# Summing the result of an attention and MLP decode step in four rows of 128 columns instead of two rows of 256

## The chip, the cores and the metric

The kernel runs on one core of a Trainium2 chip. A core has five engines with instruction queues of their own: TensorE (PE, matrix multiply, with PEld for its weight loads), VectorE (DVE), ScalarE (ACT), GpSimd (POOL) and SyncE (SP, which here only issues transfers). Transfers between HBM and the on-chip memories run on 16 DMA engines. Matmul results go to PSUM, a memory of 128 partitions in banks of 512 fp32 columns; everything else lies in SBUF, which also has 128 partitions. The metric is the device time of one execution in microseconds (us).

## What is computed

One token of width 512 goes through two branches, mixed by a gate. Branch A is attention with 32 heads of 128 over a cache of 4096 positions, branch B a small MLP with a squared ReLU. All inputs are bf16.

```python
def _A_ref(x, k_cache, v_cache, wq, wo):          # Hq = Hkv = 32, Sk = 4096, Dh = 128
    q = (x @ wq).reshape(B, Sq, Hq, Dh).transpose(0, 2, 1, 3)
    scores = jnp.einsum("bhqd,bhkd->bhqk", q, k) * (Dh ** -0.5)
    p = _softmax(scores, axis=-1)
    o = jnp.einsum("bhqk,bhkd->bhqd", p, v)
    return o.transpose(0, 2, 1, 3).reshape(B, Sq, Hq * Dh) @ wo      # wo: 4096 x 512

def _B_ref(x, w1, b1, w2, b2):                     # 512 -> 1376 -> 512
    h = x @ w1 + b1
    r = jnp.where(h > 0, h, 0)
    return (r * r) @ w2 + b2

g = _sigmoid((x * gate_w).sum(-1, keepdims=True))
return g * a + (1 - g) * b                         # 512 numbers, bf16
```

The K cache and the V cache hold 32 x 4096 x 128 bf16 numbers each, 33.5 MB.

## The kernel before

Each engine has one hand-written stream of instructions, and semaphores (`s_...`) order them. `wait_ge(s, n)` holds the engine until the semaphore has reached `n`, and `then_inc` raises it when the instruction is done (a transfer raises it by 16).

**Stream.** SyncE issues nearly all transfers on one queue, in this order: wq (L247, L248), the first K tile, w1 and w2 (L279 to L282), then K and V tiles of 4 MB in turn (`load_k`, `load_v`). There are eight groups of four heads (`NQ = 8`), each with one K tile and one V tile. A tile goes to one of three K buffers or two V buffers, and its load is issued when the buffer's last user is done. The third K buffer first holds w1, w2 and b2, so `load_k(2)` waits for the last matmul of the MLP (`s_ml`, L528). After the last V tile wo follows at L293 in four pieces, cut by `TS = [0, 20, 28, 31, 32]`: 20, 8, 3 and 1 of 32 "rows" t. Row t of wo is a 128 x 512 block.

**Scores, softmax, values.** For each group the scores are computed in three ways at once: products by GpSimd (L313) and by VectorE (L680), both summed by VectorE (L695, L689), and transposes by TensorE (L427) followed by matmuls (L441). ScalarE takes the exponentials (L358). `pv` multiplies with V into pO (L470), on four groups of partitions that begin at 0, 32, 64 and 96, and `extract` collects the heads' rows in pX.

**The result's rows.** The 512 output numbers are summed in PSUM, in a bank named pX. Before the change they lie in two places there: `accs[0]` is partitions 32 and 33, `accs[1]` partitions 0 and 1, both in columns 0 to 127. Block j (of four blocks of 128 output columns) goes to `accs[j % 2]`, as its row `j // 2`. Both rows of a place are written by each matmul: the weights are two columns, of which one is zero. The weights are cut for that from tiles of three columns with the value in the middle: `o2p` (128 x 32 x 3, the heads' outputs, of which `o2` is the middle) and `pick2` (112 x 3, ones that pick the four rows of pO). Matmuls that add into these rows are

- L520 in `mlp_out`, which puts in the scaled bias b2 (weights: `pick2`, one row);
- L535 in `mlp_cols`, which adds the MLP's rows from pvf, a copy of pO;
- L557 in `attn_rows`, for rows t = 16 to 31 of wo, four matmuls a row;
- L566 in `wide_rows`, which adds what rows t = 0 to 15 have summed in pO (L551, one matmul of 512 columns a row, on four groups of partitions) and VectorE has copied to pvf (L746).

**The end.** `busy` (L573) issues matmuls whose result nobody reads. After `regroup` (L541, with VectorE's copy into o2 at L744) come the four calls of `attn_rows`, each behind the landing of its piece of wo (`s_wo[c]`), with `wide_rows` after the first. The last matmul raises `s_acc`. Then VectorE copies `accs[0]` (L748) and ScalarE copies `accs[1]` (L385) into `ob`, partitions 32 and 33 of an SBUF tile, 256 columns, bf16. SyncE waits for both (L295), stores the two rows (L296) and waits for the store (L297).

**The start.** VectorE clears tiles, `pick2` and `o2p` among them (L636, L637), and copies the picking column into `pick2` (L640); TensorE waits for that (`s_wm`) ahead of L520.

Of the kernel before, what the change touches and what calls it, by code (L numbers as in the profile page):

```python
# [5 lines left out]
def bass_gated_mix__gqa_block_cached__dense_activation_squared_relu__decode_kernel(  # L6
# [14 lines left out]
    fp32 = mybir.dt.float32  # L21
    i32 = mybir.dt.int32
    bf16 = mybir.dt.bfloat16
    ALU = mybir.AluOpType
    ACT = mybir.ActivationFunctionType
    AX = mybir.AxisListType

    NH = 32
# [48 lines left out]
    wo_v = A_wo.rearrange("(p t) n -> p (t n)", t=32)  # L77
    w1_v = B_w1.rearrange("(p t) n -> p (t n)", t=4)
    w2_v = B_w2[0:F0, :].rearrange("(p g) n -> p (g n)", g=FG)
    out_v = out[0, 0, :].rearrange("(j p) -> j p", p=256)  # L80
    w2_x = B_w2[F1:F, :].rearrange("(q t) n -> q (t n)", t=TX)

    ctx = ExitStack()
    with ctx:
        def sb(name, shape, dt):
            return ctx.enter_context(nc.sbuf_tensor(name, shape, dt))

        def pb(name, shape, dt):
            return ctx.enter_context(nc.psum_tensor(name, shape, dt))

        def sem(name):
            return ctx.enter_context(nc.semaphore(name))
# [9 lines left out]
        kT = sb("kT", [128, NR, TC * 128], bf16)  # L102
# [9 lines left out]
        grow = sb("grow", [1, DM], bf16)  # L112
        b1r = sb("b1r", [1, F], bf16)

        ob = kT[:, 1, 0:256]
        xcol = sb("xcol", [128, 4], bf16)
        sel = sb("sel", [NH, 4, 128], bf16)
        oT = sb("oT", [NH, 128], bf16)
        o2p = sb("o2p", [128, NH, 3], bf16)
        o2 = o2p[:, :, 1]  # L120
        ident = sb("ident", [128, 128], bf16)
        identf = sb("identf", [128, 128], fp32)
        pick = sb("pick", [128, 4, 60], fp32)
        pvf = sb("pvf", [112, 512], fp32)
# [20 lines left out]
        b2r = Kt[0:1, 2, 14 * 1024:14 * 1024 + DM]  # L145
        b2g = Kt[0:1, 2, 15 * 1024:16 * 1024].bitcast(fp32)

        pick2 = sb("pick2", [112, 3], fp32)

        TT = pb("T", [128, NT * 512], fp32)  # L150
        T = [TT[:, i * 512:(i + 1) * 512] for i in range(NT)]
# [4 lines left out]
        pX = pb("pX", [128, 512], fp32)  # L156
# [5 lines left out]
        SL = pS[0:NH, 0:256].bitcast(bf16)  # L162
        H = pX[:, 160:160 + FN + TX]

        accs = [pX[32:34, 0:128], pX[0:2, 0:128]]
        O = pX[0:NH, 288:416]

        QT = pX[:, :].bitcast(bf16).rearrange("p (j d) -> p j d", d=128)
# [2 lines left out]
        def VT(i):  # L171
            return Vt[:, i % NV, :] if i < NQ - 2 else Kt[:, (i - 1) % NK, :]
# [62 lines left out]
        s_wm = sem("s_wm")  # L235
# [6 lines left out]
        s_acc = sem("s_acc")  # L242
        s_fin = sem("s_fin")
        s_out = sem("s_out")
# [5 lines left out]
        def on(engine):  # L250
            return lambda part: part(engine)

        @on(nc.sync)
        def _(eng):
            def load_k(i):
                if i >= NK:
                    eng.wait_ge(s_t, CB[i - NK + 1])
                    eng.wait_ge(s_mu, XP * (i - NK + 1))
                    eng.wait_ge(s_pm, GP * (i - NK + 1))  # L259
                if i == 2:  # L260
                    eng.wait_ge(s_ml, 1)
                eng.dma_start(Kt[:, i % NK, :], k_p[i * 128:(i + 1) * 128, :]).then_inc(s_k[i % NK], 16)

            def load_v(i):
                if i == 1:
                    eng.wait_ge(s_qr, NQ)
                    eng.wait_ge(s_h, 2)
                if i < NQ - 2:
                    if i >= NV:
                        eng.wait_ge(s_pv, i - NV + 1)  # L270
                    eng.dma_start(VT(i), v_p[i * 128:(i + 1) * 128, :]).then_inc(s_v[i % NV], 16)
                    return
                eng.wait_ge(s_t, CB[i])
                eng.wait_ge(s_mu, XP * i)
                eng.wait_ge(s_pm, GP * i)
                eng.dma_start(VT(i), v_p[i * 128:(i + 1) * 128, :]).then_inc(s_vl[i - (NQ - 2)], 16)  # L276

            load_k(0)
            eng.dma_start(w1_sb, w1_v).then_inc(s_w1, 16)  # L279
            eng.dma_start(w2a, w2_v).then_inc(s_w2, 16)  # L280
            for r in range(4):
                eng.dma_start(WX[r:QX:4, :], w2_x[r:QX:4, :]).then_inc(s_w2, 16)  # L282
            load_k(1)
            load_v(0)
            load_k(2)
            for i in range(NQ):
                if i >= 1:
                    load_v(i)
                if i + LAG < NQ:
                    load_k(i + LAG)  # L290
            eng.wait_ge(s_pv, NQ - 3)
            for c in range(NW):
                eng.dma_start(WO[:, TS[c] * DM:TS[c + 1] * DM], wo_v[:, TS[c] * DM:TS[c + 1] * DM])\  # L293
                   .then_inc(s_wo[c], 16)
            eng.wait_ge(s_fin, 2)  # L295
            eng.dma_start(out_v, ob[32:34, :]).then_inc(s_out, 16)  # L296
            eng.wait_ge(s_out, 16)  # L297

        @on(nc.gpsimd)
# [19 lines left out]
        def _(eng):  # L319
# [46 lines left out]
            for i in range(NQ + 1):  # L366
# [14 lines left out]
                if i >= 1:  # L381
                    neg_max(i - 1)
                    exps(i - 1)
            eng.wait_ge(s_acc, 1)
            eng.activation(ob[32:34, 128:256], accs[1], ACT.Copy).then_inc(s_fin, 1)  # L385

        @on(nc.tensor)
        def _(eng):
            eng.wait_ge(s_id, 2)
            for c in range(4):  # L390
                mm = eng.transpose(SL[:, c * 128:c * 128 + 128], ident[:, c:128:4], ident[:, :])
            mm.then_inc(s_sl, 1)
            eng.wait_ge(s_x, 32)
            for t in range(4):
                mm = eng.matmul(XC[:, t:t + 1], xrow[:, t:DM:4], ident[0:1, 0:1], start=True, stop=True)
# [12 lines left out]
            for j in range(NQ):  # L408
                if j >= NT:
                    wait_q(eng, j - NT)  # L410
                for t in range(4):
                    mm = eng.matmul(T[j % NT][:, :], xb[:, t, :], wq_sb[:, t, j * 512:(j + 1) * 512],  # L412
                                    start=(t == 0), stop=(t == 3))
# [77 lines left out]
            def height(n):  # L491
                return len(range(n, F1, FG)) if n < FG else QX
# [20 lines left out]
            def mlp_out():  # L513
                eng.wait_ge(s_w2, 16 * 5)
                eng.wait_ge(s_hs, 1)

                eng.wait_ge(s_wm, 3)
                eng.wait_ge(s_g, 4)
                for j in range(4):
                    eng.matmul(accs[j % 2], pick2[0:1, 1 - j // 2:3 - j // 2], b2g[:, j * 128:j * 128 + 128],  # L520
                               start=(j < 2), stop=False, skip_group_check=True)
                for n in range(FN + TX):
                    if n < FG:
                        rhs = w2a[0:height(n), n * DM:(n + 1) * DM]
                    else:
                        rhs = WX[:, (n - FN) * DM:(n - FN + 1) * DM]
                    r = 32 * (n % 4)
                    mm = eng.matmul(pO[r:r + 1, :], hs[0:height(n), n:n + 1], rhs, start=(n < 4),  # L528
                                    stop=(n >= FN + TX - 4))
                mm.then_inc(s_ml, 1)  # L530

            def mlp_cols():
                eng.wait_ge(s_mc, 1)
                for j in range(4):
                    eng.matmul(accs[j % 2], pick2[:, 1 - j // 2:3 - j // 2], pvf[0:112, j * 128:j * 128 + 128],  # L535
                               start=False, stop=False, skip_group_check=True)

            def regroup():
# [7 lines left out]
            def attn_rows(c):  # L546
                eng.wait_ge(s_wo[c], 16)
                for t in range(TS[c], TS[c + 1]):
                    r = 32 * (t % 4)
                    if t < WW:  # L550
                        mm = eng.matmul(pO[r:r + 1, :], o2[:, t:t + 1], wo_sb[:, t, :], start=(t < 4),  # L551
                                        stop=(t >= WW - 4), skip_group_check=True)
                        if t == WW - 1:
                            mm.then_inc(s_ww, 1)
                        continue
                    for j in range(4):
                        mm = eng.matmul(accs[j % 2], o2p[:, t, 1 - j // 2:3 - j // 2],  # L557
                                        wo_sb[:, t, j * 128:(j + 1) * 128], start=False,
                                        stop=(t == 31), skip_group_check=True)
                if c == NW - 1:  # L560
                    mm.then_inc(s_acc, 1)

            def wide_rows():
                eng.wait_ge(s_wc, 1)
                for j in range(4):
                    eng.matmul(accs[j % 2], pick2[:, 1 - j // 2:3 - j // 2], pvf[:, j * 128:(j + 1) * 128],  # L566
                               start=False, stop=False, skip_group_check=True)


# [46 lines left out]
            for c in range(NW):  # L616
                if c == 1:
                    busy(1)
                    wide_rows()
                attn_rows(c)  # L620

        @on(nc.vector)
        def _(eng):
# [9 lines left out]
                              identf[:, :].rearrange("p (c r) -> p c r", c=4)[:, :, 0:16]  # L633
                              .rearrange("p c (b h) -> p b h c", b=4), AX.X, ALU.add).then_inc(s_ho, 1)
            eng.memset(E[:, :, :, :], 0.0).then_inc(s_ho, 1)
            eng.memset(pick2[:, :], 0.0).then_inc(s_wm, 1)  # L636
            eng.memset(o2p[:, :, :], 0.0).then_inc(s_wm, 1)  # L637
            eng.wait_ge(s_ho, 7)
            eng.wait_ge(s_wm, 2)
            eng.tensor_copy(pick2[:, 1:2], pick[0:112, 0, 28:29]).then_inc(s_wm, 1)  # L640
            eng.wait_ge(s_sl, 1)
            eng.tensor_copy(sel[:, :, :], SL.rearrange("h (c m) -> h c m", c=4)).then_inc(s_ho, 1)
            eng.wait_ge(s_x, 32)
# [101 lines left out]
            eng.wait_ge(s_ww, 1)  # L745
            eng.tensor_copy(pvf[:, :], pO[0:112, :]).then_inc(s_wc, 1)  # L746
            eng.wait_ge(s_acc, 1)
            eng.tensor_copy(ob[32:34, 0:128], accs[0]).then_inc(s_fin, 1)  # L748


# [26 lines left out]
```

## Time and profile before

| what | us |
|---|---|
| three runs | 189.31, 189.49, 189.62 (median 189.49) |
| the profiled execution | 189.48 |
| its span, from the first to the last instruction | 188.2 |

| engine | busy us | share of the span | instructions |
|---|---|---|---|
| PE (matmul) | 109.7 | 58% | 1076 |
| PEld (weight load) | 66.2 | 35% | 1078 |
| DVE | 152.9 | 81% | 127 |
| ACT | 69.7 | 37% | 170 |
| POOL | 137.8 | 73% | 38 |

The page cuts the span into 40 slices of 4.7 us. Its row of the DMA engines' busy share, in tenths, and the row of what they moved are

```profile
DMA  7999899999999999999999999999999999999993
GB/s 265 419 432 446 375 438 438 446 425 446 430 432 439 413 425 435 425 446 432 428 425 425 432 439 421 446 432 418 432 428 432 439 425 446 421 418 424 428 394 122
```

A timeline line has the start, the length of the group from its first start to its last end, the engine, the line, the operation, the output and inputs with their shapes (a matmul's weights as rows*columns), and the number of instructions; in brackets stand the idle time before it and what ended that. "SPq" is SyncE's queue of transfers: the time there is that of issuing. A line of windows has, for each stretch, its length, each engine's busy time with the number of instructions (a matmul or weight load that straddles a border counts on both sides), the granted TensorE clock, and the share and rate of the DMA engines.

### The profile page before, as it was taken

The numbers are of one execution on the slowest core, as the hardware profiler recorded it, in microseconds if no ns is written. First come the engines' busy times: TensorE is split into PE (matmuls) and PEld (weight loads), VectorE is DVE, ScalarE is ACT, GpSimd is POOL, SyncE is SP. The second block draws the span as 40 slices with busy tenths as digits, with TensorE's granted clock in tenths as the row PEclk, the third lists the DMA queues.
The fourth block names the chain that finished last, engine by engine and source line by source line (L and its number), as shares of the span: only waits on it lengthen the run. The fifth ranks groups of instructions, "written<-read, shape, count | busy, mean of one in ns | idle before, by whom it ended". The sixth has DMA issues, their size and how long they took to land. (4 is left out here: it accounts for less than half of the span.)

```text
span 188.2 us, 2612 instructions
## 1 busy us (share of the span) xinstructions
PE 109.7 (58%) x1076; PEld 66.2 (35%) x1078; DVE 152.9 (81%) x127; ACT 69.7 (37%) x170; POOL 137.8 (73%) x38
## 2 busy tenths in 40 slices
PE   1129877787303869146806681858282648458766
PEld 1103352437103628132704181418140634213334
DVE  7112659999997999999999999999999999991022
ACT  3003484208420829404920573055405460506000
POOL 1000199998996999989998999999899989940000
PEclk9999997857655555858665555555557585858999
DMA  7999899999999999999999999999999999999993
GB/s 265 419 432 446 375 438 438 446 425 446 430 432 439 413 425 435 425 446 432 428 425 425 432 439 421 446 432 418 432 428 432 439 425 446 421 418 424 428 394 122
DMA packets 3518, 78.48 MB, mean 417 GB/s; under 512 B 410, under 2 KB 543, under 8 KB 820
## 3 DMA queue, kind: packets, MB, share of 16 engines
q1 hardware_dynamic: 3500, 78.32, 97.3%
q8 instruction: 8, 0.13, 0.3%
q14 instruction: 2, 0.02, 0.0%
q10 hardware_dynamic: 8, 0.01, 0.0%
HBM read 78.33 MB, written 0.00 MB: 416 GB/s over the span
## 5 line engine op out<-in xcount | busy, mean ns | idle before, releaser
L313 POOL TENSOR_TENSOR pg<-Kt,qb 128x2176 f32<-128x2176 bf16 x32 | 137.1, 4317 | 28.4 <-DMA Kt<-in_A_k_cache_dram 23.3
L695 DVE TENSOR_REDUCE Sb<-pg 128x17 f32<-128x2176 f32 x32 | 77.0, 2405 | 2.2 <-POOL pg L313 2.2
L427 PE MATMUL T<-ident,Kt 128*128 128x128 bf16 x256 | 27.6, 294 | 19.2 <-DMA Kt<-in_A_k_cache_dram 19.2
L341 ACT ACTIVATE kT<-T 128x1024 bf16<-128x1024 bf16 x32 | 30.8, 1030 | 17.5 <-PE T L427 17.4
L680 DVE TENSOR_TENSOR pr<-Kt,pQ 128x1792 f32<-128x1792 bf16 x16 | 32.2, 2011 | 1.9 <-DMA Kt<-in_A_k_cache_dram 1.1
L427 PEld LDWEIGHTS T<-ident,Kt 128*128 128x128 bf16 x256 | 24.0, 137 | 23.8 <-DMA Kt<-in_A_k_cache_dram 22.1
L689 DVE TENSOR_REDUCE Sb<-pr 128x14 f32<-128x1792 f32 x16 | 32.1, 2004 | 0.0
L470 PE MATMUL pO<-Vt,E 128*16 128x512 bf16 x192 | 23.0, 576 | 0.5 <-issue 0.5
L358 ACT ACTIVATE E<-Sb,nM 32x128 bf16<-32x128 f32 x32 | 18.7, 583 | 0.9
L351 ACT ACTIVATE nM<-pM 128x4 f32<-128x4 f32 x8 | 1.4, 173 | 46.5 <-PE pM L455 46.5
L441 PE MATMUL pS<-qc,kT 128*128 128x4 bf16 x256 | 11.9, 168 | 8.5 <-ACT kT L341 8.4
L412 PE MATMUL T<-Vt,kT 128*128 128x512 bf16 x32 | 10.0, 454 | 7.8 <-DMA Vt<-in_A_wq_dram 7.8
L451 PE MATMUL pM<-identf,mp 128*1 128x128 f32 x8 | 2.9, 359 | 19.3 <-DVE mp L702 19.3
L441 PEld LDWEIGHTS pS<-qc,kT 128*128 128x128 bf16 x256 | 10.4, 104 | 10.2 <-ACT kT L341 10.1
L479 PE MATMUL pX<-pvf,pick 112*32 112x128 f32 x64 | 12.8, 366 | 1.8 <-ACT pvf L364 1.8
L667 DVE CAST qb<-T 32x128 bf16<-32x128 f32 x12 | 3.4, 287 | 9.2 <-PE T L412 8.9
L333 ACT ACTIVATE qb<-T 32x128 bf16<-32x128 f32 x20 | 5.4, 268 | 14.3 <-PE T L412 13.9
L479 PEld LDWEIGHTS pX<-pvf,pick 112*32 112x32 f32 x64 | 8.6, 146 | 5.2 <-ACT pvf L364 2.5
L470 PEld LDWEIGHTS pO<-Vt,E 128*16 128x16 bf16 x192 | 6.6, 108 | 7.3 <-issue 5.7
L358 ACT ACTIVATION_READ_ACCUMULATOR E<-Sb,nM 32x1 f32 x32 | 8.2, 257 | 0.0
L451 PEld LDWEIGHTS pM<-identf,mp 128*1 128x1 f32 x8 | 0.6, 80 | 20.8 <-DVE mp L702 20.6
L455 PE MATMUL pM<-gm,onesf 1*128 1x4 f32 x16 | 4.1, 322 | 6.5 <-DVE gm L706 6.5
(81 smaller groups left out, 76.3 us busy)
## 6 DMA issues: line engine op xcount, KB each, us to landing
Kt<-in_A_k_cache_dram SPq DMA_DIRECT2D x8, 4096.0 KB, 31.2
Vt<-in_A_v_cache_dram SPq DMA_DIRECT2D x6, 4096.0 KB, 31.0
Kt<-in_A_v_cache_dram SPq DMA_DIRECT2D x2, 4096.0 KB, 31.6
Vt<-in_A_wq_dram SPq DMA_DIRECT2D x1, 3840.0 KB, 11.8
Vt<-in_A_wo_dram SPq DMA_DIRECT2D x1, 2560.0 KB, 33.2
Kt<-in_B_w_dram SPq DMA_DIRECT2D x1, 1376.0 KB, 23.9
Kt<-in_B_w_dram SPq DMA_DIRECT2D x1, 1280.0 KB
Vt<-in_A_wo_dram SPq DMA_DIRECT2D x1, 1024.0 KB, 35.2
```

What stands on the lines that cost most here:

```text
L313: eng.tensor_tensor(pg[:, n % 2, 0:g, :], Kt[:, i % NK, k * g * 128:(k + 1) * g * 128] .rearrange("p (b d) -> p b d", b=g), qb[:, i:i + 1, ...
L333: eng.activation(qb[a:b, j, :], T[j % NT][a:b, h * 128:(h + 1) * 128], ACT.Copy)\
L341: eng.activation(kT[:, n % NR, :], T[n % NT][:, :].bitcast(bf16), ACT.Copy).then_inc(s_ev, 1)
L358: eng.activation(E[a:b, j % NE, :, h], Sb[a:b, j % NS, :], ACT.Exp, bias=nM[a:b, 4 * j + h:4 * j + h + 1], scale=SCALE, accum_out=RS[a:b, ...
L412: mm = eng.matmul(T[j % NT][:, :], xb[:, t, :], wq_sb[:, t, j * 512:(j + 1) * 512], start=(t == 0), stop=(t == 3))
L427: mm = eng.transpose(T[n % NT][:, :].bitcast(bf16)[:, y * 128:(y + 1) * 128], Kt[:, i % NK, w * 128:(w + 1) * 128], ident[:, :])
L441: mm = eng.matmul(S[:, c * TC + y, :], kT[:, n % NR, y * 128:(y + 1) * 128], qc[:, 4 * i:4 * i + 4], start=True, stop=True)
L470: mm = eng.matmul(pO[r:r + 16, :], E[:, i % NE, 4 * y:4 * y + 4, :], VT(i)[:, y * 512:(y + 1) * 512], start=(y < 4), stop=(y >= NG - 4))
L479: mm = eng.matmul(O, pick[0:112, b, 28 - 4 * i:60 - 4 * i], pvf[:, b * 128:(b + 1) * 128], start=False, stop=(i == NQ - 1 and b == 3), ski ...
L680: eng.tensor_tensor(pr[:, 0:x, :], Kt[:, i % NK, a * 128:(a + x) * 128] .rearrange("p (b d) -> p b d", b=x), PQ[:, i % 4:i % 4 + 1, :].bro ...
L689: eng.tensor_reduce(Sb[:, i % NS, a:a + x], pr[:, 0:x, :], AX.X, ALU.add).then_inc(s_sd, 1)
L695: eng.tensor_reduce(Sb[:, i % NS, k * g:(k + 1) * g], pg[:, n % 2, 0:g, :], AX.X, ALU.add)\
```

## The change

The result is summed in four single rows, at partitions 0, 32, 64 and 96, one for each block of 128 output columns. A matmul's weights are one column, so `o2p` becomes `o2` (128 x 32) and `pick2` has one column; their clearing at the start goes. ScalarE's copy goes, and VectorE copies partitions 0 to 96 in one instruction of 128 columns (the partitions between the four rows with them). SyncE waits for one increment in place of two, and the store has four rows of 128 columns (256 bytes) in place of two of 256 (512 bytes). The number of matmuls that add into the rows stays the same.

```diff
-    out_v = out[0, 0, :].rearrange("(j p) -> j p", p=256)
+    out_v = out[0, 0, :].rearrange("(j p) -> j p", p=128)
...
-        ob = kT[:, 1, 0:256]
+        ob = kT[:, 1, 0:128]
...
-        o2p = sb("o2p", [128, NH, 3], bf16)
-        o2 = o2p[:, :, 1]
+        o2 = sb("o2", [128, NH], bf16)
...
-        pick2 = sb("pick2", [112, 3], fp32)
+        pick2 = sb("pick2", [112, 1], fp32)
...
-        accs = [pX[32:34, 0:128], pX[0:2, 0:128]]
+        accs = [pX[32 * j:32 * j + 1, 0:128] for j in range(4)]
...
-            eng.wait_ge(s_fin, 2)
-            eng.dma_start(out_v, ob[32:34, :]).then_inc(s_out, 16)
+            eng.wait_ge(s_fin, 1)
+            eng.dma_start(out_v, ob[0:97:32, :]).then_inc(s_out, 16)
...
-            eng.wait_ge(s_acc, 1)
-            eng.activation(ob[32:34, 128:256], accs[1], ACT.Copy).then_inc(s_fin, 1)
...
-                eng.wait_ge(s_wm, 3)
+                eng.wait_ge(s_wm, 1)
                 eng.wait_ge(s_g, 4)
                 for j in range(4):
-                    eng.matmul(accs[j % 2], pick2[0:1, 1 - j // 2:3 - j // 2], b2g[:, j * 128:j * 128 + 128],
-                               start=(j < 2), stop=False, skip_group_check=True)
+                    eng.matmul(accs[j], pick2[0:1, :], b2g[:, j * 128:j * 128 + 128],
+                               start=True, stop=False, skip_group_check=True)
...
                     for j in range(4):
-                        mm = eng.matmul(accs[j % 2], o2p[:, t, 1 - j // 2:3 - j // 2],
+                        mm = eng.matmul(accs[j], o2[:, t:t + 1],
                                         wo_sb[:, t, j * 128:(j + 1) * 128], start=False,
                                         stop=(t == 31), skip_group_check=True)
...
-            eng.memset(pick2[:, :], 0.0).then_inc(s_wm, 1)
-            eng.memset(o2p[:, :, :], 0.0).then_inc(s_wm, 1)
             eng.wait_ge(s_ho, 7)
-            eng.wait_ge(s_wm, 2)
-            eng.tensor_copy(pick2[:, 1:2], pick[0:112, 0, 28:29]).then_inc(s_wm, 1)
+            eng.tensor_copy(pick2[:, :], pick[0:112, 0, 28:29]).then_inc(s_wm, 1)
...
-            eng.tensor_copy(ob[32:34, 0:128], accs[0]).then_inc(s_fin, 1)
+            eng.tensor_copy(ob[0:97, :], pX[0:97, 0:128]).then_inc(s_fin, 1)
```

The matmuls in `mlp_cols` (L535) and `wide_rows` (L566) change as those of `attn_rows` do, with `pick2[:, :]` for their weights.

More of the change, by code (lines that the diff above doesn't have):

```diff
@@ L534, in mlp_cols @@
                 for j in range(4):
-                    eng.matmul(accs[j % 2], pick2[:, 1 - j // 2:3 - j // 2], pvf[0:112, j * 128:j * 128 + 128],
+                    eng.matmul(accs[j], pick2[:, :], pvf[0:112, j * 128:j * 128 + 128],
                                start=False, stop=False, skip_group_check=True)
@@ L565, in wide_rows @@
                 for j in range(4):
-                    eng.matmul(accs[j % 2], pick2[:, 1 - j // 2:3 - j // 2], pvf[:, j * 128:(j + 1) * 128],
+                    eng.matmul(accs[j], pick2[:, :], pvf[:, j * 128:(j + 1) * 128],
                                start=False, stop=False, skip_group_check=True)
```

## The prediction

> **What bounds the kernel now.** The time beside which the sum is made is that of the profiled execution: 189.48 us, of which 188.2 us are the span and 1.3 us lie around it. The median of the runs shown is 189.49 us, so the two may be read as one.
>
> I began with the page's rows by slice. The DMA row stands at 9 from the second slice to the last but one, and the page's queue rows give 78.3 MB on one queue, 97.3% of 16 engines' time. So nearly everything is a stream from HBM, and the engines work behind it. Then I read the chain of waits in order of time. Its end is this (start in us, length in us, what):
>
> ```profile
> 149.36 0.42 SPq L293
> 149.79 0.05 issue
> 149.84 35.22 DMA Vt<-in_A_wo_dram
> 185.05 0.04 issue
> 185.10 1.57 PE pX L557 x48
> 186.67 0.02 issue
> 186.69 0.28 DVE kT L748
> ```
>
> The last stretch of the stream is wo. When its second piece lands at 185.05, TensorE multiplies 48 times, VectorE copies, and the store follows. The change touches the 48 matmuls, the copy and the store. Read as it stands, the chain says that 1.57 us of TensorE follow the last transfer. It is not so, since wo comes in four pieces and the chain shows the first release alone. The DMA issues (size, us from issue to landing) and SyncE's own timeline give the others:
>
> ```profile
> Vt<-in_A_wo_dram SPq DMA_DIRECT2D x1, 1024.0 KB, 35.2
> Vt<-in_A_wo_dram SPq DMA_DIRECT2D x1, 384.0 KB, 35.7
> Vt<-in_A_wo_dram SPq DMA_DIRECT2D x1, 128.0 KB, 35.5
> ...
> 149.36 1.85 SPq L293 DMA_DIRECT2D Vt<-in_A_wo_dram  x4
> 187.00 0.29 SPq L296 DMA_DIRECT2D out_dram<-kT  x1
> ...
> 150.31 0.91 SPq L293 DMA_DIRECT2D Vt<-in_A_wo_dram  x2
> ```
>
> The third issue begins at 150.31 and so lands at 150.31 + 35.7 = 186.0. The fourth begins 0.43 before the end of the group, at 149.36 + 1.85 - 0.43 = 150.78, and lands at 150.78 + 35.5 = 186.3. The windows of L557 confirm it by the weight loads that start in each: 32 (8 rows of wo, four column blocks each) up to 185.98, then 12, then the last 4:
>
> ```profile
> core 0: us, PE busy (x) PEld busy (x), PEclk, DMA share, GB/s
> 185.09:185.98 0.89, 0.88 (x32) 0.87 (x32) 1.00 0.26 93
> 186.03:186.35 0.33, 0.33 (x18) 0.31 (x12) 1.00 0.00 0
> 186.35:186.66 0.30, 0.30 (x12) 0.10 (x4) 1.00 0.00 0
> 186.66:187.00 0.34, 0.00 (x0) 0.00 (x0) 1.00 0.00 0
> 187.00:188.20 1.20, 0.00 (x0) 0.00 (x0) 1.00 0.00 1
> ```
>
> So the wait that ends last in this stage is the landing of the last 128 KB at 186.3. Only the four matmuls of row 31 come after it.
>
> **The change part by part.** For the matmuls I need the step at which they follow one another in two column groups and in four. The timeline has both (start, length, what):
>
> ```profile
> 182.61 1.03 PE L551 MATMUL pO<-Vt,o2p 128*1 128x512 bf16 x16 [0.55 <-DMA Vt<-in_A_wo_dram]
> 183.47 0.61 PE L557 MATMUL pX<-Vt,o2p 128*2 128x128 bf16 x16
> ```
>
> L557 writes two column groups. One matmul lasts 0.219, so the other seven pairs take 0.61 - 0.22 = 0.39, or 0.056 a pair, for 128 columns. L551 writes four groups (partitions 0, 32, 64, 96) with one-column weights, which is what the change gives L557. One lasts 0.378, so three further sets of four take 0.65, or 0.217 a set, for 512 columns. That is 0.054 for 128 columns. The first change is thus four matmuls in the time of two, if the queue feeds them.
>
> The matmuls of the last piece: the last of the 48 ends at 185.10 + 1.55 = 186.65, so it starts at 186.43 and the pair before it at 186.375. With four groups there is one set, which starts where the first pair does or some 0.01 sooner, as the third piece's 12 are then three sets and done. The gain is one step, 0.056, to 0.065; I take 0.06. The second piece's 32 would take 8 steps in place of 16, 0.45 less; this ends in a longer wait for the landing at 186.0, and the third piece's 0.17 in one for 186.3. If both landings came before 185.1, that cover would be gone and the matmuls would be worth 24 - 12 = 12 steps, 0.67. The other bound is nothing, if sets of four are fed no faster than pairs.
>
> The other matmuls into the rows: L566 (8 records, 0.61 us, over at 185.05) ends as the second piece lands, so a shorter one waits for that landing. L535 and L520 run at 47 and 39 us. L520 stands before the matmuls of L528, whose end lets SyncE issue a K load at 42.05. The V load issued at 6.64 lands up to 43.2 later, at 49.8, so the queue holds work for another 7 us, and a change of a few tenths there is worth nothing in either direction. Without that backlog L520 would be worth at most its 1.0 us.
>
> VectorE at the start: two memsets go (0.06 and 0.14) and with them the gap before the copy at 3.13, some 0.29 in all. What hides it is the load of wq, whose first matmul is at 13.06; uncovered it would be 0.29. The smaller weights tile moves later tiles by 128 B; the rows of VectorE and GpSimd would show a cost of it, and it would have to exceed the backlog of the stream: a 4 MB load lands 31 us after its issue, though at 430 GB/s it moves in 9.8.
>
> The final copies: ScalarE's 0.267 goes. It ran from 186.69 beside VectorE's 0.283, which ended later, so nothing is saved, and SyncE waits for one increment at the same time. VectorE's copy grows from 2 to 97 partitions with the same 128 columns. The same engine's 112x512 copies from PSUM take 0.691, which is (0.691 - 0.283) / 384 = 1.06 ns a column whatever the partitions; a 128x128 cast takes 0.275. I take 0, within 0.01.
>
> The store: two rows of 512 B become four of 256 B. Nothing in the trace stores so. Issue: one row took 0.21 (the load at L321), two rows 0.29, 128 rows 0.42 to 0.44, so four rows lie between 0.29 and 0.43; the nearest row says 0.30. Transfer: from the end of the issue at 187.29 to the wait's end at 188.15 it is 0.86, of which the packets are little. In the window from 187.0 to 188.2 they fill 0.4% of 16 engines' 1.2 us, that is 0.08 us for two data packets and two completions. Half as much data a row could save 0.03 at most; two more rows starting one after the other might cost as much again. At the other end, a short row that had to be fetched and merged before it is written would add a second trip, 0.86. I take +0.03 for issue and transfer, by the nearest row, and keep -0.03 and +0.86.
>
> The Trainium skill speaks against this part: "DMA: Bandwidth & Descriptors", Specifications, has it that below 512 B a transfer is a read-modify-write. The rows stored before are just 512 B and those after are 256 B. No row here shows a store of such size, so the trace neither agrees nor differs; by that rule the case is the first rival below.
>
> The sum: 189.48 - 0.06 + 0 + 0.03 = 189.45 us.
>
> **The rivals.** First, slower: the store's short rows cost a second trip. For it: the store stands alone at the end, nothing hides it, and each row halves. Against it: packets are a small part of the 0.86. The time is 189.48 - 0.06 + 0.86 = 190.28 us. It decides from an addition of 0.06 on, and passes 0.2% from 0.44 on.
>
> Second, faster: the matmuls after 185.10 are the bound, as the chain taken alone says, and the pieces land early enough. The time is 189.48 - 0.67 + 0.03 = 188.84 us. For it speaks the single piece of 1.57 in the chain; against it the landings at 186.0 and 186.3 and the weight loads that start right behind them.
>
> Third, the change doesn't do what it says: TensorE's queue feeds one weight load and one matmul no faster than now, 0.056 / 2 = 0.028 a pair of them, and four groups run as two did. Then the gain is 0: 189.48 + 0.03 = 189.51 us. For it: L551's sets last four times as long and ask for one such feed each 0.054 only. Against it: row 31 waits for its landing, so its instructions can stand ready in the queue, and there are only four.
>
> **How the numbers follow.** What a measurement of this kernel can tell from no change is about 0.2%, 0.38 us (the three runs lie 0.31 apart). The forecast of 189.45 has 0.62, the third rival 0.14, and both are within 0.2%. The first rival has 0.12, the second 0.06. The remaining 0.06 is for a stream that lands wo more than 0.4 us earlier or later than this execution, half to each side. So faster is 0.06 + 0.03 = 0.09, within 0.2% 0.62 + 0.14 = 0.76, slower 0.12 + 0.03 = 0.15. The range runs from 189.1 to 189.95: it holds the two small cases with the spread of the runs around them, and on the upper side a store dearer by half a trip (189.45 + 0.43 = 189.88). It leaves out the whole second trip and the whole 0.67, together 0.18.
>
> **What would show it.** In the changed kernel's windows the weight loads before the second landing should still be 32, and TensorE should stand idle in front of the third and fourth pieces. From the start of the last piece's weight loads to the end of L557's matmuls there should be 0.23 us in place of 0.29. VectorE's copy should last 0.27 to 0.29. The store should be issued in 0.29 to 0.33, and from its issue to the span's end there should be 1.1 to 1.2 us, as the 1.15 of before; 1.5 or more speaks for the first rival. The forecast is wrong if the gap between the last landing of wo and the end of the matmuls shrinks by more than 0.1, or if the end moves while the landings don't.

## The result, and the profile after

| | median us | lowest to highest | runs |
|---|---|---|---|
| before | 189.41 | 189.31 to 189.62 | 13 |
| after | 189.86 | 189.68 to 189.97 | 13 |

The ratio of after to before is 1.0022, with a 95% interval of 1.0014 to 1.0030: the change costs 0.45 us. The forecast was 189.45 us, that is no change; the measured time lies inside the range of 189.1 to 189.95, but on the side that had a chance of 0.15.

The profiled span grew from 188.2 to 188.5 us. This execution's stream from HBM ended a little sooner than that of before (the last piece of wo landed at 186.17 by the trace, before at 186.32), so the spans are best compared from the last landing on. First the end of the chain of waits of the kernel after, in order of time (start in us, length in us, what):

```profile
150.55 35.30 DMA Vt<-in_A_wo_dram
185.85 0.04 issue
185.89 0.58 PE pX L554 x16
186.47 0.02 issue
186.49 0.29 DVE kT L742
```

The line numbers have moved: L554 is the matmul that was L557, L742 VectorE's copy, L295 the store. Before, the chain entered TensorE's last stretch with the landing of wo's second piece and went through 48 matmuls. Now it enters with the third piece's, since TensorE is done with the second piece early and waits. The timeline of the same stretch shows the pieces apart:

```profile
184.95 0.43 PEld L554 LDWEIGHTS pX<-Vt,o 128*1 128x1 bf16 x32 [0.56 <-DMA Vt<-in_A_wo_dram]
184.95 0.62 PE L554 MATMUL pX<-Vt,o 128*1 128x128 bf16 x32 [0.27 <-DMA Vt<-in_A_wo_dram]
185.89 0.15 PEld L554 LDWEIGHTS pX<-Vt,o 128*1 128x1 bf16 x12 [0.51 <-DMA Vt<-in_A_wo_dram]
185.89 0.55 PE L554 MATMUL pX<-Vt,o 128*1 128x128 bf16 x16 [0.33 <-DMA Vt<-in_A_wo_dram]
186.21 0.09 PEld L554 LDWEIGHTS pX<-Vt,o 128*1 128x1 bf16 x4 [0.17 <-DMA Vt<-in_A_wo_dram]
186.49 0.29 DVE L742 CAST kT<-pX 97x128 bf16<-97x128 f32 x1 [2.27 <-PE pX L554]
```

The 32 matmuls of the second piece take 0.62 us where they took 1.06 (185.10 to 186.16). Four at a time works: (0.62 - 0.22) / 7 steps is 0.057 a set of four. What is saved there turns into idle time, 0.33 ahead of the third piece. Behind the fourth piece's weight loads at 186.21 the matmuls end at 185.89 + 0.55 = 186.44, 0.23 later; before it was 0.29.

Then the store. SyncE's timeline, after:

```profile
186.81 0.59 SPq L295 DMA_DIRECT2D out_dram<-kT  x1
```

Its issue takes 0.59 in place of 0.29, and the span ends 1.66 us behind its start, in place of 1.16 (by the trace's times: 186.813 to 188.475, and 187.005 to 188.163). The whole difference, from these numbers:

| stretch | before | after | difference |
|---|---|---|---|
| weight loads of the last piece to the end of the matmuls | 0.29 | 0.23 | -0.06 |
| end of the matmuls to the store's issue (the copy lies in it) | 0.35 | 0.37 | +0.02 |
| issue of the store | 0.29 | 0.59 | +0.30 |
| end of the issue to the end of the span | 0.87 | 1.08 | +0.20 |

The sum is +0.46, against 0.45 measured over 13 runs each. So there is one loss, the store at +0.50, and the question is what of it costs: its four rows in place of two, their 256 B in place of 512 B, or that they lie 32 partitions apart.

### The profile page after: what moved, and what is told of

It reads as the page before. It is cut to its first block, busy times and chain, and to the rows that moved or that the text cites. A ratio compares the mean times of both kernels' runs of the same rounds, so it can differ in the third digit from the quotient of the medians.

```text
span 188.5 us, 2608 instructions
## 1 busy us (share of the span) xinstructions
PE 107.8 (57%) x1076; PEld 64.0 (34%) x1078; DVE 152.7 (81%) x125; ACT 69.5 (37%) x169; POOL 137.8 (73%) x38
## 5 line engine op out<-in xcount | busy, mean ns | idle before, releaser
L424 PE MATMUL T<-ident,Kt 128*128 128x128 bf16 x256 | 26.5, 286 | 18.7 <-DMA Kt<-in_A_k_cache_dram 18.7
L424 PEld LDWEIGHTS T<-ident,Kt 128*128 128x128 bf16 x256 | 23.0, 132 | 22.9 <-DMA Kt<-in_A_k_cache_dram 21.2
L467 PE MATMUL pO<-Vt,E 128*16 128x512 bf16 x192 | 22.4, 561 | 0.1
L476 PE MATMUL pX<-pvf,pick 112*32 112x128 f32 x64 | 13.6, 384 | 1.6 <-ACT pvf L363 1.6
```

The lines of the kernel that those rows point to most:

```text
L424: mm = eng.transpose(T[n % NT][:, :].bitcast(bf16)[:, y * 128:(y + 1) * 128], Kt[:, i % NK, w * 128:(w + 1) * 128], ident[:, :])
L467: mm = eng.matmul(pO[r:r + 16, :], E[:, i % NE, 4 * y:4 * y + 4, :], VT(i)[:, y * 512:(y + 1) * 512], start=(y < 4), stop=(y >= NG - 4))
L476: mm = eng.matmul(O, pick[0:112, b, 28 - 4 * i:60 - 4 * i], pvf[:, b * 128:(b + 1) * 128], start=False, stop=(i == NQ - 1 and b == 3), ski ...
```

## The experiments

The intervals are those of the ratio to the kernel before, whose runs stood beside each: 189.44 us in the first group, 189.41 in the second and third.

### Ten stores one after another

```diff
             eng.wait_ge(s_out, 16)
+            src = kT[:, 2, :]
+            eng.dma_start(scr[0:4, 0:128], src[0:97:32, 0:128]).then_inc(s_tl, 16)
+            eng.wait_ge(s_tl, 16 * 1)
+            eng.dma_start(scr[0:4, 0:128], src[0:4, 0:128]).then_inc(s_tl, 16)
+            eng.wait_ge(s_tl, 16 * 2)
...
```

> The changed kernel, and behind its store ten more stores to a scratch tensor in HBM, one after the other on SyncE's queue, each issued when the one before it has landed; they differ in rows, row size and the step between partitions (in order: 4 rows of 256 B at partitions 0, 32, 64, 96; 4 x 256 B at 0 to 3; 4 x 512 B at 0, 32, 64, 96; 2 x 512 B at 0, 1; 2 x 256 B at 0, 32; 1 x 1024 B; 3 x 512 B; 8 x 256 B; 16 x 256 B; the first again). Theory (number of rows): a store's issue takes about 0.29 us for two rows and 0.15 more for each further one, as 0.29 for two rows before, 0.59 for four after and 0.66 for the five rows of L282 say, whatever the size and the step: 0.59, 0.59, 0.59, 0.29, 0.29, 0.2, 0.44, over 0.9, and for 16 rows about 0.43 (as 128 rows) or over 2. First rival (short rows): rows of 256 B cost 0.3 more in issue and 0.2 more until they land, 512 B ones do not: 0.59, 0.59, 0.29, 0.29, 0.59. Second rival (step of 32 partitions): 0.59, 0.29, 0.59, 0.29, 0.59.

SyncE's timeline has one line for each store: start, time of the issue, line. The first is the kernel's own, and the start of the next line is some 0.02 us behind the landing of the one above it.

```profile
186.72 0.59 SPq L297 DMA_DIRECT2D out_dram<-kT  x1
188.37 0.51 SPq L300 DMA_DIRECT2D scr<-kT  x1
189.93 0.29 SPq L302 DMA_DIRECT2D scr<-kT  x1
191.11 0.51 SPq L304 DMA_DIRECT2D scr<-kT  x1
192.69 0.24 SPq L306 DMA_DIRECT2D scr<-kT  x1
193.79 0.50 SPq L308 DMA_DIRECT2D scr<-kT  x1
195.30 0.22 SPq L310 DMA_DIRECT2D scr<-kT  x1
196.39 0.24 SPq L312 DMA_DIRECT2D scr<-kT  x1
197.52 0.26 SPq L314 DMA_DIRECT2D scr<-kT  x1
198.68 0.31 SPq L316 DMA_DIRECT2D scr<-kT  x1
200.00 0.53 SPq L318 DMA_DIRECT2D scr<-kT  x1
```

Read the pairs. Four rows of 256 B take 0.51 with a step of 32 partitions (L300) and 0.29 without (L302). With the step, 512 B cost as much as 256 B (L304), and two rows as much as four (L308). Without it 1, 2, 3, 8 and 16 rows take 0.22 to 0.31, whatever their size. From issue to the next issue it is 1.56 to L300's successor and 1.18 to L302's: the step costs 0.38, of which 0.22 is issue. The theory of the number of rows falls, and the rival of the step holds in every line, though here the issue with a step is some 0.08 shorter than the 0.59 of the kernel's own store.

### Steps from 1 to 64

> The changed kernel, and behind its store eleven more to a scratch tensor, each issued when the one before it has landed. In order: 2 rows of 512 B with a step between their partitions of 1, 2, 4, 8, 16, 32 and 64; 5 rows of 256 B with step 4; 2 partitions (step 1) with two separate pieces of 256 B each; 4 rows of 256 B with step 1 into a contiguous kilobyte; 2 rows of 512 B with step 1 again. Theory (a step other than 1 makes the issue longer): issue 0.25 for step 1, 0.50 for every other step alike, from issue to landing 1.09 and 1.5 us; five rows with step 4 about 0.55. Rival (it is the step of 32, that is another group of 32 partitions): steps 2 to 16 take 0.25 as step 1, and 32 and 64 take 0.50. Rival (the rows in HBM not being contiguous adds): the contiguous four rows are cheaper than the 0.29 measured with gaps. The pieces: 0.5 or more if any second dimension counts, 0.25 if it is the partitions' step alone.

The same construction, with these sources (the third to last has two pieces of 256 B in each of two partitions):

```diff
+            eng.dma_start(scr[0:2, 0:256], src[0:2, 0:256]).then_inc(s_tl, 16)
+            eng.dma_start(scr[0:2, 0:256], src[0:3:2, 0:256]).then_inc(s_tl, 16)
...
+            eng.dma_start(scr[0:2, 0:256], src[0:65:64, 0:256]).then_inc(s_tl, 16)
+            eng.dma_start(scr[0:5, 0:128], src[0:17:4, 0:128]).then_inc(s_tl, 16)
...
```

```profile
188.52 0.28 SPq L300 DMA_DIRECT2D scr<-kT  x1
189.65 0.65 SPq L302 DMA_DIRECT2D scr<-kT  x1
191.32 0.56 SPq L304 DMA_DIRECT2D scr<-kT  x1
192.90 0.54 SPq L306 DMA_DIRECT2D scr<-kT  x1
194.47 0.54 SPq L308 DMA_DIRECT2D scr<-kT  x1
196.04 0.47 SPq L310 DMA_DIRECT2D scr<-kT  x1
197.54 0.47 SPq L312 DMA_DIRECT2D scr<-kT  x1
199.04 0.72 SPq L314 DMA_DIRECT2D scr<-kT  x1
200.82 0.25 SPq L316 DMA_DIRECT2D scr<-kT  x1
201.94 0.26 SPq L318 DMA_DIRECT2D scr<-kT  x1
203.09 0.23 SPq L320 DMA_DIRECT2D scr<-kT  x1
```

Step 1 takes 0.28 and at the end again 0.23; the steps 2, 4, 8, 16, 32 and 64 between them all take 0.47 to 0.65, and from issue to the next issue 1.50 to 1.67 in place of 1.10 to 1.13. So every step tried other than 1 has the cost, and the rival of crossing into another group of 32 partitions falls. The issues with a step were expected to be alike at 0.50, and they are not: they fall from 0.65 to 0.47 along the list. As the step grows with the place in the list, these runs do not tell which of the two does that. Five rows with step 4 take 0.72, which was expected at 0.55: with a step the number of rows may count as well, though not from two to four. Four rows of step 1 into one contiguous kilobyte take 0.26, and 1.15 to the next issue, little less than the 1.18 with gaps.

### The step alone, added and removed

Undone in the kernel after, and put into the kernel before:

```diff
-            eng.dma_start(out_v, ob[0:97:32, :]).then_inc(s_out, 16)
+            eng.dma_start(out_v, ob[0:4, :]).then_inc(s_out, 16)
```

> The changed kernel with its store alone altered: it reads partitions 0 to 3 in place of 0, 32, 64 and 96, four rows of 256 B as after (only the first of them is a row of the result). Theory (the step is the cost): issue 0.29 to 0.35, from issue to the end 1.16 to 1.22 us, which is 0.02 to 0.08 more than before; with 0.06 less behind the last landing and 0.01 more in the copy the ratio is 0.9998 to 1.0002. Rival (number or length of rows): the ratio stays at 1.0022.

```diff
-            eng.dma_start(out_v, ob[32:34, :]).then_inc(s_out, 16)
+            eng.dma_start(out_v, ob[32:97:64, :]).then_inc(s_out, 16)
```

> The kernel before with its store alone altered: it reads partitions 32 and 96 in place of 32 and 33, two rows of 512 B as before (the second is not a row of the result). Theory (the step is the cost): issue 0.58 in place of 0.29, from issue to the end 1.55 to 1.65 in place of 1.14, ratio 1.0022 to 1.0027. Rival (number or length of rows): ratio 1.

| kernel | median us | ratio | interval | issue | start of issue to end |
|---|---|---|---|---|---|
| after, step 1 | 189.49 | 1.0004 | 0.9996 to 1.0013 | 0.30 | 1.21 |
| before, step 64 | 189.85 | 1.0024 | 1.0015 to 1.0033 | 0.59 | 1.62 |

SyncE's line of the first, and then of the second:

```profile
186.95 0.30 SPq L295 DMA_DIRECT2D out_dram<-kT  x1
```

```profile
186.90 0.59 SPq L296 DMA_DIRECT2D out_dram<-kT  x1
```

Without the step the kernel after can't be told from the kernel before, though its rows are as many and as short. With it the kernel before is as slow as the kernel after, though its two rows of 512 B are what they were. By the medians, taking the step out of the kernel after gives back 0.37 (189.86 to 189.49), and putting it into the kernel before costs 0.44 (189.41 to 189.85). So the step makes the loss of 0.45, as far as the scatter of the runs tells. Four short rows by themselves cost 1.21 - 1.16 = 0.05, about what the matmuls gain.

The trace also shows where in the store the time goes. The first increment of the store's semaphore comes 0.16 us after the end of the issue in the kernels without a step (before and step 1), and 0.42 after it in those with one (after and step 64). From there to the last increment it is 0.68 and 0.71 without a step, and 0.63 and 0.58 with one. So the added time stands in the issue and between it and the first increment, and the rest of the store is not longer. What fills that time, the profile does not show.

### Fewer rows, and two queues

```diff
-            eng.dma_start(out_v, ob[0:97:32, :]).then_inc(s_out, 16)
+            eng.dma_start(out_v[0:2, :], ob[0:33:32, :]).then_inc(s_out, 16)
```

> The changed kernel, which stores only the first two of its four rows; the second half of the output isn't written. Theory (number of rows): issue 0.29 us, the end comes 0.5 us sooner than after: ratio to the kernel before about 0.9997. Rival (short rows): the two rows are as short as the four, so ratio about 1.002. Rival (step of 32 partitions): the same 1.002.

The same line, and besides it the other two rows on ScalarE's queue:

```diff
+            eng.wait_ge(s_fin, 1)
+            eng.dma_start(out_v[2:4, :], ob[64:97:32, :]).then_inc(s_out, 16)
```

> The changed kernel with its store split: SyncE stores the first two rows, ScalarE's queue the other two, both when VectorE's copy is done. Theory (number of rows in one issue): two issues of about 0.29 us side by side, from their start to the span's end 1.15 us as before in place of 1.65; the kernel keeps its 0.06 from the matmuls: ratio about 0.9997 (189.35 to 189.4 us). Rival (short rows): ratio about 1.0025, as after.

Half the store leaves the time where it was: 189.86 us, 1.0024 (1.0014 to 1.0033). Two queues are no better: 190.13 us, 1.0035 (1.0021 to 1.0048). Both expectations of the theory of rows missed. The timelines show why, first with half the store and then with two queues:

```profile
187.03 0.59 SPq L295 DMA_DIRECT2D out_dram<-kT  x1
```

```profile
187.01 0.59 SPq L295 DMA_DIRECT2D out_dram<-kT  x1
187.02 0.58 ACTq L384 DMA_DIRECT2D out_dram<-kT  x1
```

Two rows with a step are issued in 0.59, as four are, and now two queues pay it. They also land later still (1.79 from issue to end, in the kernel after 1.66): the trace has two increments at 188.59 and 188.60 and the other two 0.18 later, at 188.77. What the two stores share was not tried.

### Four pieces out of two partitions

```diff
-    out_v = out[0, 0, :].rearrange("(j p) -> j p", p=256)
+    out_v = out[0, 0, :].rearrange("(j c p) -> j c p", c=2, p=128)
...
-        ob = kT[:, 1, 0:256]
+        ob = kT[:, 1, 0:320]
...
-            eng.dma_start(out_v, ob[32:34, :]).then_inc(s_out, 16)
+            eng.dma_start(out_v, ob[32:34, :].rearrange("q (c p) -> q c p", c=2)[:, :, 0:128]).then_inc(s_out, 16)
...
-            eng.activation(ob[32:34, 128:256], accs[1], ACT.Copy).then_inc(s_fin, 1)
+            eng.activation(ob[32:34, 160:288], accs[1], ACT.Copy).then_inc(s_fin, 1)
```

> The kernel before, in which the store alone differs: the same two partitions, but two separate pieces of 256 B from each, so four pieces of 256 B. Theory (number of partitions, that is of engines, sets the issue): two partitions, issue about 0.29 us, ratio to the kernel before within 0.05% of 1. Rival (short rows are the cost): ratio about 1.0025, issue 0.59 or a landing 0.3 later. If pieces count and not partitions, issue 0.59 as well, and the first run's 4 x 512 B tells which.

It took 189.99 us, 1.0031 (1.0019 to 1.0042), with an issue of 0.73:

```profile
186.84 0.73 SPq L296 DMA_DIRECT2D out_dram<-kT  x1
```

Its first increment, too, comes 0.42 after the issue's end, so this store pays in the same two places although its partitions are adjacent. Taken alone this would have spoken for the rival of short rows. The run of steps says otherwise: two partitions with two pieces of 256 B each, adjacent partitions too, are issued in 0.25 there (L316). The two differ on the HBM side: here the four pieces are one contiguous kilobyte in HBM, which the trace records as four pieces in one dimension, there they are recorded as two by two, as they lie in SBUF. It would fit that the two sides have to be brought to one shape, but that was not tried by itself.

### Without a step, in the kernel after

Two ways of keeping the four column groups and storing without a step. Four stores of one row each:

```diff
-            eng.dma_start(out_v, ob[0:97:32, :]).then_inc(s_out, 16)
-            eng.wait_ge(s_out, 16)
+            for j in (0, 1):
+                eng.dma_start(out_v[j:j + 1, :], ob[32 * j:32 * j + 1, :]).then_inc(s_out, 16)
+            eng.wait_ge(s_out, 64)
...
+            eng.wait_ge(s_fin, 1)
+            for j in (2, 3):
+                eng.dma_start(out_v[j:j + 1, :], ob[32 * j:32 * j + 1, :]).then_inc(s_out, 16)
```

> The changed kernel with its store cut into four stores of one row each, two on SyncE's queue and two on ScalarE's. Theory (the step is the cost, a single row has none): each issue about 0.22 us, the second of a queue begins some 0.25 to 0.3 after the first, so from the first issue to the end 1.08 + 0.25 = 1.33 to 1.4 us; the ratio is 1 + (0.2 to 0.26 - 0.05) / 189.4 = 1.0008 to 1.0011, between before and after. Rival (short rows): at or above 1.0022.

It took 189.86 us, 1.0023 (1.0013 to 1.0033), as long as the kernel after: a miss. SyncE's and ScalarE's queues:

```profile
186.84 0.65 SPq L296 DMA_DIRECT2D out_dram<-kT  x2
186.85 0.52 ACTq L386 DMA_DIRECT2D out_dram<-kT  x2
```

Each issue is short, but two follow each other on a queue (0.65 for SyncE's two together), and in the trace the four rows land at 187.90, 188.08, 188.25 and 188.43, one by one at 0.18. From first issue to the end it is 1.62.

One row, brought together by copies that change partition (the store is then `ob[:, :]`, one row of 512 columns):

```diff
+            eng.wait_ge(s_acc, 1)
+            for j in (2, 3):
+                eng.activation(ob[:, j * 128:(j + 1) * 128], accs[j], ACT.Copy).then_inc(s_fin, 1)
...
-            eng.tensor_copy(ob[0:97, :], pX[0:97, 0:128]).then_inc(s_fin, 1)
+            for j in (0, 1):
+                eng.tensor_copy(ob[:, j * 128:(j + 1) * 128], accs[j]).then_inc(s_fin, 1)
```

> The changed kernel with its four rows brought together in one partition: VectorE copies two of the accumulators and ScalarE the other two, each 1 x 128 into its quarter of one row of 1024 B in partition 0, and the store is that one row. Theory (the step of the partitions is the cost, and only that): the store has no step and from issue to the end it takes 1.08 to 1.15 us, as the 1.14 of before; each engine's second copy adds 0.2 to 0.29 ahead of it; the matmuls keep their 0.06. Ratio 1 + (0.2 to 0.29 - 0.06 - 0.03) / 189.4 = 1.0006 to 1.0011, better than after (1.0022) by 0.2 to 0.3 us and not better than before. If the second copies overlapped the first fully it would be 0.9997 and beat both.

It took 189.64 us, 1.0015 (1.0005 to 1.0024): by the medians 0.22 less than the kernel after, though the two intervals overlap, and not better than the kernel before. The ratio is a little above the 1.0006 to 1.0011 expected. The end of its timeline:

```profile
186.41 0.56 ACT L385 ACTIVATE kT<-pX 1x128 bf16<-1x128 f32 x2 [12.37 <-PE pX L557]
186.41 0.59 DVE L746 CAST kT<-pX 1x128 bf16<-1x128 f32 x2 [2.25 <-PE pX L557]
187.03 0.28 SPq L295 DMA_DIRECT2D out_dram<-kT  x1
```

The second copies don't overlap the first, so the copies take 0.59 in place of 0.28. The store behaves as before, 1.16 from issue to end. So +0.31 stands against -0.06, which is 0.25 by the trace and 0.23 by the medians. No variant beat the kernel before.

## Why the prediction missed

**What was right.** That the chain's 1.57 us of TensorE are not behind the last transfer: TensorE now idles 0.33 ahead of the third piece, and the 0.23 from the last weight loads to the last matmul is the forecast number, so the matmuls gave 0.06. The second rival (0.67 from the matmuls) is out, and the third (four groups fed no faster than two) as well: sets of four follow at 0.057. VectorE's copy of 97 partitions lasts 0.29, within the 0.01 that was kept for it, and ScalarE's copy saved nothing. The changes at the start and in the middle show nothing at the end: wo's last piece landed 0.15 sooner in this execution, but the landing scatters by more than that: from 186.08 to 186.39 in the profiles of the eight kernels with the new start, and from 186.15 to 186.32 in the three with the old one.

**The step that failed** is the store's price: "so four rows lie between 0.29 and 0.43; the nearest row says 0.30", and with it "I take +0.03 for issue and transfer". Measured are 0.59 for the issue and +0.50 in all, mis-sized by 0.47 us. That is the whole miss, from 189.45 to 189.86 with a median of before that lies 0.07 below the profiled execution. The rows were ordered by their number, and every row used had adjacent partitions. Even among those the number set no such bounds: in the same trace the four loads of one row at L320 to L323 were issued in 0.52, 0.21, 0.27 and 0.27, and loads of 128 rows in 0.33 to 0.44, one of them (L280) in 0.53. The change's other novelty, the step of 32 in `ob[0:97:32, :]`, was put at nothing without a reason. Yet the trace of before had rows with a step: the four loads at L282, five partitions four apart, which its timeline shows as

```profile
3.17 2.94 SPq L282 DMA_DIRECT2D Kt<-in_B_w_dram  x4
```

and its view of that line as

```profile
L282 SPq DMA_DIRECT2D Kt<-in_B_w_dram x4: 657/672/809, 3.2 to 5.5; - x4
```

So one issue took 0.66 to 0.81, with a median of 0.67, far outside the 0.43 given as the upper end, and it was left out. With it the step could have added 0.67 - 0.29 = 0.38 to the issue, and the sum would have been about 189.8. These loads differ from the store in more than the step (five rows of 5 KB), so the row would have given a bound and not the cause.

The measured 189.86 lies inside the stated range by luck: the upper end was set by half a second trip, and no second trip is what cost the time.

**The first rival** had the right place and the right side: the store stands alone at the end with nothing to hide it. Its mechanism and price (short rows, a second trip of 0.86) are not what happened. The sign named for it, 1.5 or more from the store's issue to the span's end, came with 1.66; but a step gives that sign as well, so it could not tell the two apart. The Trainium skill's rule for it ("DMA: Bandwidth & Descriptors", Specifications, below 512 B a read-modify-write) can be set beside the stores of step 1 now: four rows of 256 B took 1.15 to 1.18 from issue to next issue, two rows of 512 B 1.10 to 1.13. At this size at most 0.08 (1.18 - 1.10) can be put down to short rows, and what a large store of short rows would take, no run here shows.

## What to carry to other kernels

Nothing hides a store at the very end, so its shape is part of the price of any layout that feeds it: here the layout gained 0.06 us in the matmuls and lost 0.50 in the store that has to collect its rows. When an operation is priced by the nearest row of a trace, list everything in which it differs from the rows before (number, length, step, shape on both sides) and look for a row that shares each, above all one that contradicts the bound. And a group that the chain of waits shows behind one landing may still contain later landings: compute each piece's before taking its length for a gain.

## What the runs showed of the hardware

- A store of two rows from SBUF to HBM whose partitions are not adjacent was issued in 0.47 to 0.65 us in place of 0.23 to 0.28, and took 1.50 to 1.67 in place of 1.10 to 1.13 from its issue to the next one, for each step tried from 2 to 64. The added time lies in the issue and in the 0.42 (in place of 0.16) from its end to the first increment of the store's semaphore.
- A step between partitions is not the only shape with that price: four pieces of 256 B out of two adjacent partitions, which form one contiguous kilobyte in HBM, were issued in 0.73, again with 0.42 to the first increment. Why is open.
- With adjacent partitions the number of rows hardly matters to the issue: 1 to 16 rows were issued in 0.22 to 0.31. From issue to the next issue it was 1.09 for one row of 1 KB and 1.32 for sixteen of 256 B.
- Four stores of single rows, two on each of two queues, landed one after the other at 0.18 us.
- VectorE's copy begins 0.050 to 0.053 us behind the last matmul in the eight kernels with four column groups (186.443 to 186.494 after) and 0.041 to 0.043 in the three with two (186.652 to 186.695 before, 186.545 to 186.587 with step 64). The copy's own shape is not the cause, since the kernel with one-row copies has 0.051. The ends of the matmuls are modelled by the profile. The Trainium skill's "TensorE: Matmul & The Clock Gate", The cost: per-tile semaphore tail, has a term of 4.7 ns a tile; two more tiles would be an estimated 9 ns, and the trace's difference of 8 to 10 ns agrees. The formula as a whole would give an estimated 61 ns for two tiles and one increment, more than the 42 ns measured here.
